# Down-projection in seven products of 256 columns in the second pass, with combinations made by GpSimd and SyncE in source order

## The chip, the cores and the metric

The kernel runs on one core of one Trainium2 chip. The core has TensorE (PE in the profile, its weight loads PEld), VectorE (DVE), ScalarE (ACT), GpSimd (POOL), SyncE (SP, which here issues the DMA transfers) and the DMA engines. Each engine works through its own instructions in order, and semaphores make one engine wait for another. The metric is the device time of one execution in microseconds; less is better.

## The reference

A transformer block on 2048 rows of 512: adaptive layer norm, attention of 32 query heads on 8 cached key/value heads over the last 512 cached positions, a gated residual, a second adaptive layer norm, and a gated feed-forward with F = 1792:

```python
def _B_ref(x, w_gate, w_up, w_down):
    return (_gelu(x @ w_gate) * (x @ w_up)) @ w_down
...
h = _layernorm(x, axis=-1) * (1 + ca) + sa
x = x + ga * _A_ref(h, A_k_cache, A_v_cache, A_wq, A_wo)
h = _layernorm(x, axis=-1) * (1 + cb) + sb
x = x + gb * _B_ref(h, B_w_gate, B_w_up, B_w_down)
```

Inputs and output are float32.

## The kernel before, in words

**Numbers.** Every matmul works on float16. A float32 operand is split in a high half (a ScalarE copy) and a low half (the difference, on VectorE or GpSimd), and a product is three matmuls: low by high, high by low, high by high (`mm3`, L85 to L88).

**Order.** Up to the first feed-forward sets, the program is a table of due positions: `at(position, function)` puts work there, and the block under `tc.manual_schedule()` (from L1383) runs the positions in turn; inside it every engine's instructions keep the order in which the source makes them. After it, the feed-forward loop (L1478 to L1494) makes its instructions in a similar order, but the framework's scheduler then orders each engine's queue, SyncE's included, by times of its own. `T` is the number of the attention's steps; positions T − 18 and so on are counted from its end.

**Feed-forward.** The hidden width is cut into blocks of 128, taken in pairs: NP = 7 pairs, two passes over them. The first pass (n = 0 to 6) does rows 0 to 1023, the second (n = 7 to 13) rows 1024 to 2047. Each n has two sets, q = 2n for the gate and q = 2n + 1 for the up projection. A set multiplies 1024 rows by 256 weight columns as a 2 × 2 block product in seven products (Winograd's form of Strassen), each of 6 matmuls of 512 columns: 42 matmuls. `ORDER` is the order of the seven. Three PSUM chains take them: `fa` (tag `s`, 2 buffers; `qa`, 1 buffer, for q = 0), `fb` and `fc` (tag `acc`, NACC = 5 buffers). The left combinations of the activations are tiles b11, b21, b22 and t1 to t4. Those of the second half of the rows are made in sets 7 to 10: SyncE loads four blocks (`combos`, L466), GpSimd makes differences (L478) and low halves (L343), ScalarE high halves (L339). The right combinations of the weights were made once, during the attention, and wait in DRAM (`store`, L310 to L312); `set_fetch` (L1094) and `fetch` (L314, L315) bring them back, four tiles a set, in buffers w0, w1, w2 and x3 of two each.

**After a product.** `keep` (L783 to L785) copies a chain from PSUM with ScalarE; VectorE adds two parts (L1161). For a gate set `gelu` runs on 128 × 512: square on ScalarE (L1168), VectorE (L1171), tanh on ScalarE (L1174), VectorE (L1178). For an up set VectorE multiplies by the gate (L1189), ScalarE takes the high half (L1191), VectorE the low (L1192): the tiles `at`, for keys 11, 21, 12 and 22 (two blocks of hidden columns by two quarters of the rows).

**Down-projection.** For each n `y_tasks` (L840 to L856) makes eight tasks, one for each row tile of 128: 2 × 3 matmuls of 512 columns in a bank `py`, with the scaled weight blocks `wo` (two a pair, fetched from what `prep_wd`, L1277, stored), and one VectorE addition onto `acc` (L852). They wait in `nexty`; `y_next` (L1444) takes one after products 1, 2, 5 and 6 of the next sets. The eight `acc` tiles are a half's rows. When the first pass is done with a row tile, `f_final` (L1473) stores it to the output and loads the second half's tile in its place.

**The seam with the attention.** `attn_final` (L858) stores each finished row tile `y` (L860) and loads the tile that is to come next in `acc` (L94). `ln_tile` (L420) loads a row tile `xs` from `y` (L427) for the second layer norm: statistics on VectorE (L352, L354, L356), the normalised rows (L434), transposes on TensorE (L439, `pln`), scaled copies (L447), stores of them (`hs`).

Of the kernel before, what the change touches and what calls it, by code (L numbers as in the profile page):

```python
# [63 lines left out]
def block_kernel(ctx: ExitStack, tc: tile.TileContext, x, kT, v, wq, wo, wg, wu, wd, cT, wc, wm, out):  # L64
# [709 lines left out]
    def banks(st, tags):  # L774
        def bk(k):
            def get():
                if k not in st:
                    st[k] = bank(*tags[k])
                return st[k]
            return get  # L780
        return bk
# [360 lines left out]

    NP = NF // 2
    NQ = 4 * NP
    B, A, G = {}, {}, {}

    def set_srcs(q):
        n, m = divmod(q, 2)
# [6 lines left out]
    def f_items(q, hold=None):  # L1155
        n, m = divmod(q, 2)
        st = {}
        done = set()

        def add(k, src):  # L1160
            nc.vector.tensor_tensor(st[k], st[k], st[src], op=ALU.add)  # L1161

        def gelu(key, src):
            b = {}

            def square():
                b["sq"] = pool.tile([P, QB], F32, tag="k", name="sq", bufs=2)
                nc.scalar.activation(b["sq"], src, AF.Square, scale=col("finv", f_scale(q)))  # L1168

            def inner():  # L1170
                nc.vector.scalar_tensor_tensor(b["sq"], b["sq"], 1.0 / GELU_A, src, op0=ALU.add, op1=ALU.mult)  # L1171

            def tanh():
                nc.scalar.activation(b["sq"], b["sq"], AF.Tanh, scale=col("tsc", f_scale(q)))  # L1174

            def outer():
                dst = tmp("fg") if key == "21" else src
                nc.vector.scalar_tensor_tensor(dst, b["sq"], 1.0, src, op0=ALU.add, op1=ALU.mult)  # L1178
                G[n, key] = dst

            return square, inner, tanh, outer

        def result(key, src):
            if m == 0:
                for step in gelu(key, src):
                    step()
            else:
                g = G.pop((n, key))
                nc.vector.scalar_tensor_tensor(g, g, 0.5 * GU, src, op0=ALU.mult, op1=ALU.mult)  # L1189
                t = pair("ot", "at", NOT)  # L1190
                nc.scalar.activation(t[:, 0, :], g, AF.Copy)  # L1191
                nc.vector.tensor_tensor(t[:, 1, :], g, t[:, 0, :], op=ALU.subtract)  # L1192
                A[n, key] = t
# [30 lines left out]
        return with_posts(("f", q), 2 + q // (2 * NP), banks(st, tags), after)  # L1224

    def f_spread_at(q):
        return (lambda m: f_spread(f_scale(q), m)) if q < 2 * NP else None
# [79 lines left out]
    for n in range(NP):  # L1307
# [1 line left out]
        prep_set(2 * n, b)  # L1309
        prep_set(2 * n + 1, b + 13)  # L1310
        prep_wd(n, b + 18)
    for q, ps_ in ((0, (T - 18, T - 17, T - 16, T - 15)), (1, (T - 8, T - 7, T - 3, T))):
        for k, pos in zip((0, 3, 2, 1), ps_):
            at(pos, lambda q=q, k=k: set_fetch(("f", q), ("f", q), k))

# [41 lines left out]
    def pushes(u, y):  # L1357
# [79 lines left out]
    def all_of(ts):  # L1437
        for g, post in ts:
            g()
            if post:  # L1440
                post()
                run(("d", now[0] + 1))

    def y_next():  # L1444
        if nexty:
            all_of(nexty.pop(0))

    ORDER = (1, 2, 6, 7, 5, 4, 3)

    def f_at(q, k, *fns):  # L1450
        at(("f", q, k), *fns)

    for n in range(2 * NP):
        for k in range(2):
            f_at(2 * n + 1, 2 * k, lambda n=n, k=k: WO.update({("f", n, k): fetch(("wd", n % NP, k), get_wo())}))
    for q in range(2, NQ):
# [16 lines left out]
    def f_final(ti):  # L1473
        nc.sync.dma_start(rows_of(out, ti), acc[ti])
        if ti < 2 * QT:
            load_acc(ti + 2 * QT, y1[ti + 2 * QT])

    f_done = {(0, k) for k in ORDER} | {(1, 1), (1, 2), (1, 6)}  # L1478
    for q in range(NQ):
        n, m = divmod(q, 2)  # L1480
        its = items(NG + q) if q < 2 else f_items(q)
        for k, pk in enumerate(ORDER):
            if (q, pk) not in f_done:
                all_of(its[pk])
            run(("f", q, k))
            if k in (1, 2, 5, 6):
                y_next()
        if m == 1:
            for qi, (a, b) in enumerate((("11", "21"), ("12", "22"))):
                for i in range(QT):  # L1490
                    nexty.append(y_tasks((2 * (n // NP) + qi) * QT + i, [lambda n=n, a=a: A[n, a], lambda n=n, b=b: A[n, b]],
                                         [("f", n, 0), ("f", n, 1)], col("dysc", n % NP), f_final if n % NP == NP - 1 else None))
    while nexty:
        y_next()  # L1494
    assert not later, list(later)


# [32 lines left out]
```

## Time and profile before

| | |
|---|---|
| runs | 1783.33, 1782.06, 1777.99 us |
| median | 1782.06 us |
| the profiled execution's own time | 1783.9 us |
| its span in the trace | 1782.1 us |
| its mean granted TensorE clock | 0.998 |
| HBM read, written | 133.83 MB, 59.90 MB |

A row of a group reads: line, engine, operation, output <- inputs, partitions × elements and types, count; after the bar the group's busy time in us and the mean duration of one in ns; after the second bar the engine's idle time just before these instructions, and what ended most of it. A row of a timeline has start and duration in us; a bracket at its end holds the idle time before and its releaser. A row of the chain of waits has start, duration and piece; "issue" is time in which the engine waited for nothing that the profile shows. Matmuls are pipelined, so their starts tell more than their durations. The attention ends, and the feed-forward takes the whole TensorE, at about 1346 us.

### The profile page before, as it was taken

To read this page: it belongs to the slowest core of one execution; us is meant where nothing else is said; L and a number is where in the kernel's file an instruction comes from. 1 tells how busy PE (TensorE), PEld (TensorE's weight loads), DVE (VectorE), ACT (ScalarE), POOL (GpSimd) and SP (SyncE) were. 2 spreads that over 40 slices of the span, in tenths; PEclk is the share of its full clock that TensorE was granted. 3 is DMA by queue.
4 is the path that set the end of the run, shared out by engine and by line. 5 is a ranking of instruction groups with operands and counts; after the bars stand their busy time and mean duration, and the time that the engine had idled before them with its cause. 6 is when DMAs were issued, how large, how long until landed. Compare 5 with 4: busy or idle time off the path is not lost.

```text
span 1782.1 us, 26030 instructions
## 1 busy us (share of the span) xinstructions
PE 1735.6 (97%) x8112; PEld 796.0 (45%) x8114; DVE 1442.5 (81%) x2517; ACT 1211.1 (68%) x2814; POOL 874.2 (49%) x1095
## 2 busy tenths in 40 slices
PE   7899999999999999999999999999999999999999
PEld 5444444444444444444444444444444444444444
DVE  7888888888888888888887888787885758676676
ACT  6877787878878777687877777777773455344342
POOL 4879878776788863236575375464420023000000
PEclk9999999999999999999999999999999999999999
DMA  7999999999999989999999999999985643252321
GB/s 232 197 189 236 204 224 207 222 214 206 218 211 210 211 175 182 228 223 212 217 208 211 237 203 212 212 196 203 187 184 141 215 126 99 73 177 84 86 69 56
DMA packets 663274, 329.71 MB, mean 185 GB/s; under 512 B 553184, under 2 KB 575968, under 8 KB 663136
## 3 DMA queue, kind: packets, MB, share of 16 engines
q1 hardware_dynamic: 662848, 327.53, 80.0%
q8 instruction: 64, 1.05, 0.3%
q14 instruction: 74, 0.61, 0.1%
q10 hardware_dynamic: 288, 0.52, 0.1%
HBM read 133.83 MB, written 59.90 MB: 109 GB/s over the span
## 4 chain that ended last, share of the span: by engine, by line
PE 67%; DVE 14%; ACT 7%; POOL 4%; DMA 4%; issue 4%; SPq 1%; POOLq 0%; ACTq 0%; DVEq 0%
PE py L86 7%; PE py L88 7%; PE py L87 7%; PE ps L86 4%; PE ps L88 4%; PE ps L87 4%; PE po L86 4%; PE po L88 4%; PE po L87 4%; DVE p L901 3%; DVE nm L875 3%; PE fa L86 2%; PE fa L88 2%; PE fa L87 2%; ACT ee L884 2%
## 5 line engine op out<-in xcount | busy, mean ns | idle before, releaser
L884 ACT ACTIVATE ee<-ps,nm 128x512 f32<-128x512 f32 x512 | 350.8, 685 | 244.6 <-DVE nm L875 234.6
L901 DVE SCALAR_TENSOR_TENSOR p<-ee,rr,p 128x512 f16<-128x512 f32 x512 | 464.8, 908 | 0.2
L875 DVE TENSOR_REDUCE nm<-ps 128x1 f32<-128x512 f32 x512 | 348.7, 681 | 67.2 <-PE ps L88 65.8
L896 ACT ACTIVATE p<-ee,rr 128x512 f16<-128x512 f32 x512 | 365.5, 714 | 12.8 <-DMA pt<-p 11.9
L86 PE MATMUL ps<-k,qt 128*128 128x512 f16 x512 | 194.3, 380 | 21.5 <-DVE qt L644 15.2
L86 PE MATMUL po<-pt,v 128*128 128x512 f16 x512 | 194.0, 379 | 2.8 <-DVE p L901 1.3
L86 PE MATMUL py<-wo,ot 128*128 128x512 f16 x512 | 194.1, 379 | 2.1 <-DVE ot L644 2.0
L88 PE MATMUL ps<-k,qt 128*128 128x512 f16 x512 | 194.2, 379 | 0.0
L87 PE MATMUL ps<-k,qt 128*128 128x512 f16 x512 | 194.2, 379 | 0.0
L88 PE MATMUL py<-wo,ot 128*128 128x512 f16 x512 | 194.0, 379 | 0.0
L87 PE MATMUL py<-wo,ot 128*128 128x512 f16 x512 | 194.0, 379 | 0.0
L88 PE MATMUL po<-pt,v 128*128 128x512 f16 x512 | 194.0, 379 | 0.0
L87 PE MATMUL po<-pt,v 128*128 128x512 f16 x512 | 194.0, 379 | 0.0
L892 DVE RECIPROCAL rr<-rr 128x2 f32<-128x2 f32 x256 | 41.5, 162 | 118.0 <-ACT rr L889 116.6
L87 PEld LDWEIGHTS <-w 128*128 128x128 f16 x728 | 71.4, 98 | 91.7 <-issue 7.6
L88 PEld LDWEIGHTS <-w 128*128 128x128 f16 x728 | 71.5, 98 | 86.8 <-issue 1.6
L86 PEld LDWEIGHTS <-w 128*128 128x128 f16 x728 | 71.4, 98 | 86.4 <-issue 1.3
L852 DVE SCALAR_TENSOR_TENSOR acc<-py,dysc,acc 128x512 f32<-128x512 f32 x112 | 81.7, 746 | 34.6 <-PE py L88 32.1
L362 POOL TENSOR_TENSOR rs<-rs,nhalf 128x1 f32<-128x1 f32 x32 | 19.2, 599 | 168.6 <-DVE rs L356 166.0
L884 ACT ACTIVATION_READ_ACCUMULATOR ee<-ps,nm 128x1 f32 x512 | 100.7, 197 | 0.0
L852 DVE SCALAR_TENSOR_TENSOR acc<-py,ysc,acc 128x512 f32<-128x512 f32 x128 | 94.6, 739 | 2.5 <-PE py L88 2.5
L86 PE MATMUL py<-wo,at 128*128 128x512 f16 x224 | 84.9, 379 | 3.0 <-DVE acc L852 1.9
(263 smaller groups left out, 3818.8 us busy)
## 6 DMA issues: line engine op xcount, KB each, us to landing
w<-kept SPq DMA_DIRECT2D x123, 256.0 KB, 3.1
wo<-kept SPq DMA_DIRECT2D x60, 256.0 KB, 3.2
raw<-in_wo SPq DMA_DIRECT2D x56, 256.0 KB, 3.5
kept<-stage SPq DMA_DIRECT2D x56, 256.0 KB, 3.5
kept<-w SPq DMA_DIRECT2D x39, 256.0 KB, 3.3
rw<-in_wq SPq DMA_DIRECT2D x38, 256.0 KB, 3.8
hs<-hf SPq DMA_DIRECT2D x32, 256.0 KB, 2.7
pt<-p SPq DMA_TRANSPOSE x512, 3.6
```

Of the source, the lines that this page charges most:

```text
L86: nc.tensor.matmul(ps, llo, rhi, start=first, stop=False, skip_group_check=chain)
L87: nc.tensor.matmul(ps, lhi, rlo, start=False, stop=False, skip_group_check=chain)
L88: nc.tensor.matmul(ps, lhi, rhi, start=False, stop=last, skip_group_check=chain)
L362: nc.gpsimd.tensor_tensor(st["rs"], st["rs"], nhalf, op=ALU.pow)
L852: nc.vector.scalar_tensor_tensor(acc[ti], st["p"], by, acc[ti], op0=ALU.mult, op1=ALU.add)
L875: nc.vector.tensor_reduce(nm, E[t]["ps"], axis=AX.X, op=ALU.max, negate=True)
L884: nc.scalar.activation(e, E[t]["ps"], AF.Exp, bias=E[t]["nm"], scale=1.0, accum_out=sm[:, t % 2:t % 2 + 1])
L892: return lambda: nc.vector.reciprocal(r, r)
L896: nc.scalar.activation(p16[:, 0, :], E[t]["e"], AF.Copy, scale=E[t]["r"])
L901: nc.vector.scalar_tensor_tensor(p16[:, 1, :], E[t]["e"], E[t]["r"], p16[:, 0, :], op0=ALU.mult, op1=ALU.subtract)
```

## The change

The down-projection of n = 7 to 12 (`seven(n)`) (two quarters of the rows by two hidden blocks, times two hidden blocks by two halves of 256 output columns) becomes a 2 × 2 block product in seven products too. Products are 128 × 256; each of the seven is 2 × 2 × 3 = 12 matmuls, 84 for an n where there were 48 of 512 columns. They run in two groups (x = 0, 1), each with two row tiles of either quarter of the rows: 6 matmuls a product and group.

- *Left combinations.* After the up set's product "12", `y_sums` makes four sums of 512 columns on GpSimd, then four splits (ScalarE copy, GpSimd difference), due after products of the next set: s1 to s4. The product with the gate goes into the up part's tile or a `qt` tile instead of the gelu's tile; "12" is not split on VectorE.
- *Right combinations.* `wd_combined(n)` for n = 0 to 5 in the first pass loads the two raw blocks again, scales them with GpSimd (a gate tile and two multiplications), makes four differences of 256 columns and two splits on it, and stores two tiles. In the second pass four `wo` tiles are fetched for such an n instead of two.
- *After the products.* Three of seven ("keep") are copied from PSUM by ScalarE with the scale into a tile `yk` and added to `acc` by GpSimd, two additions of 256 columns each; the other additions, of 256 columns too, stay on VectorE but are put off to behind the next task's matmuls (`defer`). For an n that is `seven` that makes 6 ScalarE copies, 12 GpSimd additions and 16 VectorE additions.
- *Banks.* Chain `fa` takes its bank in turn from `qa`, `s`, `s` (`chain_tag`), and chain a of the down-projection shares that turn.
- *Order.* SyncE's whole program is put in source order (the line `manual_schedule(engines={... SP})`); the other engines are ordered as before. Set 2 and the first `wo` tiles are fetched near the attention's end, the loads of `acc` for the second half are put off (`load_later`), and `y_next` runs after every product once n > 7 or while such loads wait.

The last pair (n = 13) and the whole first pass keep the plain down-projection. TensorE's instructions in all: 216 matmuls more.

```diff
+    def seven(n):
+
+        return NP <= n < 2 * NP - 1
...
+    def y_sums(n):
+        g11, g21, g12, g22 = (R.pop((n, k)) for k in ("11", "21", "12", "22"))
+        nc.gpsimd.tensor_tensor(g22, g12, g22, op=ALU.add)
+        nc.gpsimd.tensor_tensor(g12, g11, g12, op=ALU.subtract)
+        nc.gpsimd.tensor_tensor(g11, g22, g11, op=ALU.subtract)
+        nc.gpsimd.tensor_tensor(g21, g21, g11, op=ALU.subtract)
...
+            nc.scalar.activation(t[:, 0, :], src, AF.Copy)
+            nc.gpsimd.tensor_tensor(t[:, 1, :], src, t[:, 0, :], op=ALU.subtract)
...
+        for i, (k, src) in enumerate(((0, g22), (1, g11), (3, g21), (2, g12))):
+            at(("f", 2 * n + 2, 1 + i), lambda k=k, src=src: split(k, src))
...
-        tags = {"a": ("s", "fa", 2) if q else ("qa", "fa", 1), "b": ("acc", "fb", NACC), "c": ("acc", "fc", NACC)}
+        tags = {"a": chain_tag, "b": ("acc", "fb", NACC), "c": ("acc", "fc", NACC)}
...
+        return (("qa", "fa", 1), ("s", "fa", 2), ("s", "fa", 2))[(chains[0] - 1) % 3]
...
+    for k in range(2):
+        at(T - 1 + 2 * k, lambda k=k: WO.update({("f", 0, k): fetch(("wd", 0, k), get_wo())}))
+    for q, ps_ in ((0, (T - 18, T - 17, T - 16, T - 15)), (1, (T - 8, T - 7, T - 3, T)), (2, (T + 2, T + 3, T + 4, T + 5))):
...
+    ctx.enter_context(tc.manual_schedule(engines={mybir.EngineType.SP}))
...
     def y_next():
         if nexty:
+            fns = defer[:]
+            defer.clear()
             all_of(nexty.pop(0))
+            for fn in fns:
+                fn()
+        if len(load_later) > 2 or load_later and not nexty:
+            t = load_later.pop(0)
+            load_acc(t, y1[t])
...
+    YPROD = {1: ("a", "11", 0, 0, "keep", 0, 0), 2: ("b", "21", 1, 0, "add", 0, 0), 5: ("c", "s1", 2, 0, "add", 1, 1),
+             6: ("a", "s2", 3, 1, "keep", 0, 1), 3: ("c", "s4", 1, 1, "add", 0, 1), 7: ("a", "s3", 2, 1, "keep", 1, 1),
+             4: ("a", "22", 3, 0, "add", 1, 0)}
+
+    def y_seven(n, x):
...
+            for ii in range(2):
+                sl = slice((2 * x + ii) * P, (2 * x + ii + 1) * P)
+                mm3(st[ch][:, 256 * ii:256 * ii + 256], A[n, a][:, 0, sl], A[n, a][:, 1, sl], w[:, 0, rs], w[:, 1, rs],
+                    k in (1, 2, 5) and ii == 0, k in (2, 3, 4) and ii == 1, True)
...
+            if what == "keep":
+                src = pool.tile([P, 512], F32, tag="rw", name="yk", bufs=NRW)
+                nc.scalar.activation(src, st[ch], AF.Copy, scale=by)
+            for ii in range(2):
...
+                if what == "keep":
+                    nc.gpsimd.tensor_tensor(t, t, s_, op=ALU.add)
+                else:
+                    defer.append(lambda t=t, s_=s_: nc.vector.scalar_tensor_tensor(t, s_, by, t, op0=ALU.mult, op1=ALU.add))
...
+    def wd_combined(n, q):
...
+        def combine():
+            tt(st[0][:, l], st[0][:, r], st[0][:, l])
+            tt(st[0][:, r], st[1][:, r], st[0][:, r])
+            tt(st[1][:, r], st[1][:, r], st[0][:, l])
+            tt(st[1][:, l], st[1][:, l], st[1][:, r])
...
+        def keep_it(k):
+            store(("wd", n, 2 + k), st["o", k])
+
+        for d, fn in enumerate((lambda: (load(0), load(1)), nop, gate, lambda: scaled(0), lambda: scaled(1), combine,
+                                lambda: parts(0), lambda: parts(1), nop, lambda: keep_it(0), lambda: keep_it(1))):
+            f_at(q + d // 7, d % 7, fn)
...
+    for n in range(1, 2 * NP):
+        for k in range(4 if seven(n) else 2):
+            f_at(2 * n + 1, 1 + k if seven(n) else 2 * k, lambda n=n, k=k: WO.update({("f", n, k): fetch(("wd", n % NP, k), get_wo())}))
+    for n in range(NP - 1):
+        wd_combined(n, 2 * n + 3)
+    for q in range(3, NQ):
...
-            load_acc(ti + 2 * QT, y1[ti + 2 * QT])
+            load_later.append(ti + 2 * QT)
...
-            if k in (1, 2, 5, 6):
+            if n > NP or k in (1, 2, 5, 6) or load_later:
                 y_next()
-        if m == 1:
+        if m == 1 and seven(n):
+            f_at(q + 1, 2, lambda n=n: nexty.extend(y_seven(n, 0) + y_seven(n, 1)))
+        elif m == 1:
```

More of the change, by code (lines that the diff above doesn't have):

```diff
@@ L1188, in result @@
                 g = G.pop((n, key))
[L1189 to L1193, printed above, removed]
+                dst = src if seven(n) and key != "21" else get_qt32() if seven(n) else g
+                nc.vector.scalar_tensor_tensor(dst, g, 0.5 * GU, src, op0=ALU.mult, op1=ALU.mult)
+                R[n, key] = dst
+                if not seven(n) or key != "12":
+                    t = pair("ot", "at", NOT)
+                    nc.scalar.activation(t[:, 0, :], dst, AF.Copy)
+                    nc.vector.tensor_tensor(t[:, 1, :], dst, t[:, 0, :], op=ALU.subtract)
+                    A[n, key] = t
+                if seven(n) and key == "12":
+                    y_sums(n)
         def out_(key, src):
@@ L1451, in f_at, with load, gate, scaled @@
         at(("f", q, k), *fns)
[L1453 to L1456, printed above, removed]
+    def wd_combined(n, q):
+        st = {}
+        l, r = slice(0, 256), slice(256, 512)
+        def load(k):
+            st[k] = raw("raw")
+            nc.sync.dma_start(st[k], wd[(2 * n + k) * P:(2 * n + k + 1) * P, :])
+        def gate():
+            st["g"] = pool.tile([P, D], F32, tag="gs", name="gs", bufs=1)
+            pool_ts(st["g"], rows[5], col("dsc", n))
+        def scaled(k):
+            nc.gpsimd.tensor_tensor(st[k], st[k], st["g"], op=ALU.mult)
+        def tt(o, a, c):
+            nc.gpsimd.tensor_tensor(o, a, c, op=ALU.subtract)
+        def combine():
[3 more added lines that the diff above has]
+            tt(st[1][:, l], st[1][:, l], st[1][:, r])
+        def parts(k):
+            st["o", k] = pair("p16", "wdc", NP16)
+            halves(st["o", k], st[k])
+        def keep_it(k):
[9 more added lines that the diff above has]
+    for q in range(3, NQ):
         for k, at_ in ((0, 2), (3, 2), (1, 3), (2, 4)):
@@ L1494, in block_kernel @@
         y_next()
+    for fn in defer:
+        fn()
     assert not later, list(later)
```

30 lines of the change are left out of this document (27 added, 3 removed).

## The prediction

> **What bounds the kernel now.** I read the page's totals first, then the engines by stretch from the last attention step on, then single waits.
>
> ```profile
> span 1782.1 us, 26030 instructions
> PE 1735.6 (97%) x8112; PEld 796.0 (45%) x8114; DVE 1442.5 (81%) x2517; ACT 1211.1 (68%) x2814; POOL 874.2 (49%) x1095
> ```
>
> TensorE (PE) bounds the whole, so every term below is either TensorE work or TensorE waiting. By stretch (start to end, length; then busy time and count of PE, PEld, DVE, ACT and POOL; then clock and DMA):
>
> ```profile
> 1345.00:1375.00 30.00, 27.13 (x118) 11.90 (x119) 15.16 (x25) 9.83 (x16) 0.95 (x1) 0.94 0.43 116
> 1375.00:1410.00 35.00, 32.80 (x154) 15.02 (x153) 25.11 (x48) 11.24 (x22) 2.74 (x5) 1.00 0.66 212
> 1410.00:1455.00 45.00, 45.00 (x222) 22.06 (x221) 32.92 (x55) 26.01 (x54) 2.25 (x3) 1.00 0.47 139
> 1455.00:1490.00 35.00, 32.03 (x146) 13.90 (x145) 23.12 (x31) 17.08 (x31) 28.46 (x21) 1.00 0.43 132
> 1490.00:1757.00 267.00, 267.00 (x1239) 121.06 (x1238) 186.34 (x284) 108.20 (x171) 0.00 (x0) 1.00 0.31 91
> 1757.00:1782.10 25.10, 20.82 (x96) 8.98 (x94) 16.65 (x25) 5.75 (x10) 0.00 (x0) 1.00 0.23 84
> ```
>
> From 1490 to 1757 TensorE never waits: 267.00/1239 = 0.2155 us for a 512-column matmul. Fewer columns there shorten the run one for one. GpSimd (POOL) does nothing there; VectorE is busy 70%, ScalarE 41%. A pair of feed-forward sets with a down-projection is 84 + 48 = 132 matmuls, 28.4 us. Ahead of 1490 TensorE idles 2.87 + 2.20 + 0 + 2.97 = 8.0 us: the only other time to be won.
>
> **The matmuls.** In six of seven pairs of the second pass 84 matmuls of 256 columns replace 48 of 512. Neither pass has a 256-column product with this shape, so its price is bounded: half of 0.2155 is 0.108; if the weight load cannot hide, 0.108 + 0.098 = 0.206.
>
> ```profile
> 1447.83 0.38 PE L88 MATMUL py<-wo,at 128*128 128x512 f16 x1
> 1448.04 0.60 PE L439 MATMUL pln<-ident,xs 128*128 128x128 f32 x4
> 1448.48 0.38 PE L86 MATMUL fb<-b,w 128*128 128x512 f16 x1
> L88 PEld LDWEIGHTS <-at 128*128 128x128 f16 x153 | 15.0, 98 | 18.0
> ...
> ```
>
> (0.38 is pipelined duration; starts count.) The nearest row is the four transposes, each with weights of its own: 1448.48 − 1448.04 = 0.44, or 0.11 each, so weights do change every 0.11 us. I take 0.109, just over half. Each n: 48 × 0.2155 − 84 × 0.109 = 1.19; six make **−7.1** (−7.7 at half). Break-even is 10.34/84 = 0.123.
>
> The Trainium skill, "TensorE: Matmul & The Clock Gate", under "The mechanism", says that a weight load overlaps running matmuls only when it goes to another row group, and these loads fill all rows. Here the 98 ns loads stand between 512-column matmuls at 0.2155, so they are hidden; the trace disagrees, and no run here shows 256 columns. By the rule each of them would take 0.206, the last rival's case.
>
> **SyncE in source order, and the waits early in the first pass.** Before, VectorE held normalisations whose rows had not arrived:
>
> ```profile
> 1346.40 0.76 DVE acc L852
> ...
> 1348.22 2.75 DMA y<-acc
> ...
> 1351.04 3.02 DMA xs<-y
> ...
> 1354.08 0.70 DVE bn L352
> ```
>
> ```profile
> 1360.22 0.38 PE L88 MATMUL fa<-b,w 128*128 128x512 f16 x1
> 1362.94 0.58 PE L86 MATMUL fa<-t,w 128*128 128x512 f16 x1 [2.33 <-ACT fg L785]
> 1363.32 0.63 PE L87 MATMUL fa<-t,w 128*128 128x512 f16 x1
> ```
>
> ```profile
> 1397.09 5.27 DMA xs<-y
> ...
> 1405.64 0.67 DVE acc L852
> ...
> 1406.36 0.66 PE pln L439 x4
> ```
>
> While bn waited for xs, the gelu steps queued behind it on VectorE, ScalarE's copies behind those, and TensorE stood 2.33 us; the matmuls after that start 0.43 apart instead of 0.2155, and seven of them lose 1.5. At 1402 the same wait costs the 2.20 idle of 1375 to 1410. In the changed program's order the first bn stands behind attention's last adds, and y8 to y15 stores and all eight acc loads stand ahead of the xs loads on SyncE. So gelu no longer queues behind a bn that waits; I leave 0.7 for copies late by themselves: 2.33 + 1.5 + 2.2 − 0.7 = **−5.3**. Bounds: −6.5, if all of the idle goes, to 0, if the later xs loads (sixteen transfers further back) give it back.
>
> At the turn of the passes, the acc loads and output stores precede set fetches in SyncE's order: TensorE waits there for nothing now; sixteen issues of 0.42 us are spread over pairs; I take **+0.7** (0 to 2).
>
> ```profile
> 1385.08 0.42 SPq L94 DMA_DIRECT2D acc<-y  x1
> ```
>
> **GpSimd in the first pass.** For six pairs it scales and combines two wd blocks. By the rows of such forms:
>
> ```profile
> L1245 POOL TENSOR_TENSOR rw<-rw 128x256 f32<-128x256 f32 x56 | 48.5, 866 | 4.1
> L1298 POOL TENSOR_TENSOR raw<-raw,gs 128x512 f32<-128x512 f32 x14 | 18.8, 1344 | 0.6
> L153 POOL TENSOR_TENSOR stage<-rw,stage 128x512 f16<-128x512 f32 x42 | 55.0, 1310 | 3.5
> L152 POOL TENSOR_SCALAR stage<-rw 128x512 f16<-128x512 f32 x42 | 30.5, 725 | 2.5 <-DMA kept<-stage 0.2
> ...
> L478 POOL TENSOR_TENSOR cb<-cb 128x512 f32<-128x512 f32 x8 | 11.5, 1437 | 27.7 <-DMA cb<-hs 27.7
> L343 POOL TENSOR_TENSOR t<-cb,t 128x512 f16<-128x512 f32 x8 | 11.0, 1379 | 0.0
> ```
>
> 0.73 (gate) + 2 × 1.344 + 4 × 0.866 + 2 × (0.725 + 1.310) = 11.0 us a pair. Elsewhere GpSimd is near idle, but in sets 7 to 10 it also makes the second half's combinations: a pair's four L478 and seven L343, 15.4, so 26.4 of 28.4. SyncE meanwhile waits in its queue for the combined pieces' halves before it may issue the next set's w0, then the following cb loads; ScalarE waits for t1 to t4. A fetch needs 3.1 us. Laying the rows end to end, set 7's fetch is in time, set 8's 0.5 late, set 9's 2 to 4, while the 2.97 idle of today partly falls in the same places. I take **+2** (0 to +9, if set 9's lateness is paid, GpSimd overruns, and the clock halves once).
>
> ```profile
> w<-kept SPq DMA_DIRECT2D x123, 256.0 KB, 3.1
> ```
>
> **The second pass's helpers.** Each n now gives GpSimd four sums (1.344), four splits (1.310) and twelve 256-column adds (0.866): 21.0 of the new 27.2 us; ScalarE ten copies more, less one split.
>
> ```profile
> L852 DVE SCALAR_TENSOR_TENSOR acc<-py,dysc,acc 128x512 f32<-128x512 f32 x78 | 56.9, 747 | 26.9 <-PE py L88 24.5 <-DMA x<-kept 1.6
> L1192 DVE TENSOR_TENSOR at<-fg,at 128x512 f16<-128x512 f32 x38 | 26.2, 689 | 9.6 <-ACT at L1191 8.3
> L1171 DVE SCALAR_TENSOR_TENSOR sq<-sq,fg 128x512 f32<-128x512 f32 x29 | 20.0, 688 | 3.6 <-ACT sq L1168 3.6
> ...
> L785 ACT ACTIVATE fg<-fa 128x512 f32<-128x512 f32 x29 | 17.2, 594 | 46.4 <-PE fa L88 46.4
> ```
>
> Ten copies add some 5.9 us to ScalarE's 11.5 (108.20/267 of 28.4): hidden. VectorE changes eight adds of 0.747 for sixteen of 256 columns, between 0.37 and 0.75; in the ratio of GpSimd's two sizes (0.866/1.344) 0.48. 7.7 − 6.0 − 0.69 = +1.0 on 19.9: hidden.
>
> Not hidden by totals alone is the handover. After a pair's last product VectorE needs three steps (3 × 0.69 = 2.1), then GpSimd two sums, the keep adds that stand between in its order, and the split of s1. In the changed program's order the pairs have 0, 2, 2, 0, 4 and 4 adds there, the last also a third sum. With two: 2.1 + 2 × 1.344 + 2 × 0.866 + 1.310 = 7.8; over the pairs 6.1, 7.8, 7.8, 6.1, 9.6, 10.9. Up to its first matmul on s1 TensorE's order holds, for the third pair, 36 matmuls of 512 columns and 24 of 256, 36 × 0.2155 + 24 × 0.109 = 10.4; counted so, 7.3, 8.2, 10.4, 7.8, 11.0, 11.7. The margins are 0.4 to 2.6, the later operands' wider, ScalarE's copies of s not in them: I take 0.4 a pair, **+2.4** (0 to +12, if each is 2 late).
>
> **Tail.** Now one 0.75 add follows the last matmul. The plain last pair remains, but with deferred adds of the pair before it ahead on VectorE and two more y tasks drawn earlier or later:
>
> ```profile
> 1778.08 0.23 PE py L88
> ...
> 1778.34 0.75 DVE acc L852
> ```
>
> Two 256 and two 512 adds may stand there, 2 × 0.48 + 2 × 0.75 − 0.75 = 1.7: **+1.5** (0 to 2).
>
> **Sum.** −7.1 − 5.3 + 0.7 + 2 + 2.4 + 1.5 = −5.8 on the profiled execution. Its span of 1782.1 and 1.8 us around it make 1783.9, 1.84 over the median 1782.06; so 1782.06 − 5.8 = **1776.3 us**.
>
> **Rivals.** *SyncE's order gives nothing.* The attention's stores and acc loads delay xs by as much as bn was moved. For: at 1397 the xs transfer itself took 5.27 us, and more transfers now share that time. Against: the bn that waits no longer stands ahead of the gelu steps at all. The −5.3 vanishes: 1781.6.
>
> *GpSimd and VectorE slow each other, and what GpSimd makes comes late* (the slower case). Where both work, VectorE's step L1171 takes longer, and GpSimd's difference has a long end (min/median/max):
>
> ```profile
> L1171 DVE SCALAR_TENSOR_TENSOR sq<-sq,fg 128x512 f32<-128x512 f32 x12 | 9.9, 821 | 1.9 <-ACT sq L1168 1.7
> L478 POOL TENSOR_TENSOR cb<-cb x27: 1262/1271/1781, 103.6 to 1482.6; 128x512 f32<-128x512 f32 x27
> ```
>
> 821/688 = 1.19 and 1781/1271 = 1.40. With these on VectorE's and GpSimd's parts the six handovers become 8.1, 10.5, 10.5, 8.1, 13.0 and 14.8, late by 0.8, 2.3, 0.1, 0.3, 2.0 and 3.1: 8.6 instead of 2.4. The three of 2 us and more are as long as the stall that lost the clock at 1362: 3 × 1.5 = 4.5. In sets 7 to 10 GpSimd's 11.0 becomes 15.4, 2.4 over the 28.4 in two pairs: 4.8. Together 15.5: 1792. It decides from where GpSimd is slowed by about 1.1. Against: in the busy stretch L478 has a mean of 1.437, only 1.13 of 1.271, and my prices are means that hold some of it.
>
> The Trainium skill, "SBUF — State Buffer", under "Who interferes with whom", has a VectorE instruction with two SBUF inputs and a GpSimd instruction that reads SBUF exclude each other for their whole length. The two rows above agree in kind. By it the splits and products of VectorE, twelve of 0.69, add 8.2 to GpSimd's 21.0 of 27.2, which no longer fits: the rival's time or more.
>
> *Weight loads stand between 256-column matmuls*: 504 × (0.206 − 0.109) = +49, 1825.
>
> **How the numbers follow.** The forecast has 0.50, by itself 1770 to 1781 (the first pass's and the handover's terms at nothing and the matmuls at half, or one of the two up by 4); SyncE's order idle 0.15; the mutual slowing 0.27; weight loads 0.04; 0.04 for a gain above all bounds. Some 0.3% (5.35 us) is what a measurement can tell here: faster is below 1776.7, slower above 1787.4. Of the forecast's 0.50, 0.32 lies below; with the 0.04 and 0.02 of the idle order, faster 0.38. Same: 0.18 of the forecast, 0.13 of the idle order, 0.02 of the slowing: 0.33. Slower: 0.29. The range, 1766 to 1793, leaves out the weight loads and the upper part of the slowing.
>
> **What would show it.** Right: 256-column matmuls start 0.108 to 0.110 apart; no 2 us stall near 1360 and 1402 and a full clock; GpSimd at 70 to 80% in the second pass with its 512 sums near 1.34; TensorE idle under 4 us there, ahead of as operands. Wrong: waits of TensorE on w fetches or on ScalarE t around sets 8 to 10 beyond 4 us, GpSimd's sums above 1.5, VectorE's 0.69 steps above 0.8, starts above 0.123 apart, or a clock under 1.00 after 1490.

## The result, and the profile after

The changed kernel takes 1793.08 us (median of 6 runs, 1789.39 to 1795.03) against 1781.97: a ratio of 1.0065 (95% interval 1.005 to 1.008), 0.65% slower where 0.3% faster was forecast, and just past the far end of the range (1766 to 1793). The profiled execution has a span of 1791.8 us. Its page, totals:

```profile
span 1791.8 us, 26801 instructions
...
PE 1736.0 (97%) x8330; PEld 817.1 (46%) x8330; DVE 1473.9 (82%) x2559; ACT 1241.7 (69%) x2868; POOL 1068.2 (60%) x1281
```

The same view by stretch as before the change; the first pass now ends near 1600:

```profile
1345.00:1375.00 30.00, 29.04 (x134) 13.10 (x135) 15.02 (x23) 9.52 (x16) 0.00 (x0) 1.00 0.47 132
1375.00:1410.00 35.00, 35.00 (x169) 16.65 (x168) 26.26 (x47) 15.21 (x29) 6.65 (x8) 1.00 0.64 212
1410.00:1455.00 45.00, 40.54 (x195) 19.10 (x194) 35.12 (x58) 21.43 (x43) 19.36 (x22) 1.00 0.38 123
1455.00:1520.00 65.00, 57.02 (x241) 24.14 (x239) 45.47 (x56) 27.78 (x46) 49.84 (x41) 0.92 0.43 142
...
1600.00:1660.00 60.00, 57.01 (x333) 32.09 (x331) 43.16 (x69) 32.95 (x54) 35.28 (x35) 1.00 0.45 149
1660.00:1765.00 105.00, 102.68 (x621) 60.32 (x619) 85.18 (x138) 60.73 (x100) 78.64 (x76) 1.00 0.29 95
```

The first two rows are won: 0.96 us of idle where there were 2.87 + 2.20, and the full clock. The next two lose 4.46 + 7.98, the second of them with a clock of 0.92. The second pass, which never waited, now idles 2.99 + 2.32. TensorE's waits in the first pass, from its timeline:

```profile
1361.03 0.38 PE L86 MATMUL fa<-t,w 128*128 128x512 f16 x1 [0.69 <-ACT fg L785]
...
1418.82 0.39 PE L86 MATMUL fa<-b,w 128*128 128x512 f16 x1 [1.50 <-DMA w<-kept]
...
1446.74 0.39 PE L86 MATMUL fa<-b,w 128*128 128x512 f16 x1 [1.34 <-DMA w<-kept]
...
1478.39 0.58 PE L86 MATMUL fa<-t,w 128*128 128x512 f16 x1 [3.38 <-ACT u L785]
...
1514.90 0.61 PE L86 MATMUL fa<-b,w 128*128 128x512 f16 x1 [2.54 <-DMA w<-kept]
```

The wait of 2.33 us before the gelu result near 1360 is down to 0.69. New are waits for weights (`w<-kept`) that the kernel before does not have; from 1345 to 1600 they make 5.8 of the 14 us that TensorE waits, and waits for ScalarE's copies (L785) make 6.4. SyncE's timeline shows why the weights come late:

```profile
1410.06 0.57 SPq L427 DMA_DIRECT2D xs<-y  x1
1415.62 0.32 SPq L312 DMA_DIRECT2D kept<-wdc  x1
1415.99 0.42 SPq L315 DMA_DIRECT2D w<-kept  x1
...
1457.22 0.33 SPq L312 DMA_DIRECT2D kept<-wdc  x1
1457.64 1.05 SPq L315 DMA_DIRECT2D w<-kept  x2
1458.78 1.89 SPq L475 DMA_DIRECT2D cb<-hs  x4
...
1461.19 15.63 SPq L1544 DMA_DIRECT2D raw<-in_wd  x2
...
1495.61 14.44 SPq L1544 DMA_DIRECT2D raw<-in_wd  x2
1510.09 0.43 SPq L315 DMA_DIRECT2D wo<-kept  x1
1510.57 0.43 SPq L315 DMA_DIRECT2D w<-kept  x1
```

From 1410.6 to 1415.6 SyncE issues nothing: the store of a combined block waits for GpSimd, and the fetch that TensorE waits for at 1418 stands right behind it. At 1457 the same kind of store stands ahead of the loads for the second half's combinations. At 1461 and 1495 two loads of raw blocks take 15.63 and 14.44 us to issue: the ring of five raw buffers holds four blocks of those combinations, so the second load waits until ScalarE and GpSimd let one go, and the fetch at 1510.57 is the one that TensorE waits for until 1514.90.

The longest wait, 3.38 us until 1478.39, is for a ScalarE copy, and two things stand ahead of that copy. ScalarE waits 7.0 us for the late `cb` loads, until 1464.41 (4.5 us, until 1459.67, before). Then VectorE's gelu steps, which ScalarE's copies follow, are slow while GpSimd makes the combinations:

```profile
1468.98 1.43 DVE L1197 SCALAR_TENSOR_TENSOR sq<-sq,fg 128x512 f32<-128x512 f32 x1 [0.44 <-ACT sq L1194]
1470.34 1.75 DVE L1216 SCALAR_TENSOR_TENSOR fg<-fg,fu 128x512 f32<-128x512 f32 x1
```

With GpSimd idle, in the second pass of the kernel before, such steps take 0.69 us. After the waits at 1478 and 1515 the matmuls start 0.43 us apart for a while instead of 0.2155: half clock.

The second pass by groups, 1600 to 1765 (mean ns behind the busy time):

```profile
L1527 POOL TENSOR_TENSOR acc<-acc,yk 128x256 f32<-128x256 f32 x62 | 51.3, 852 | 79.9 <-ACT yk L1522 79.9
L1529 DVE SCALAR_TENSOR_TENSOR acc<-py,dysc,acc 128x256 f32<-128x256 f32 x64 | 29.0, 476 | 9.0 <-POOL acc L1527 8.3 <-PE py L88 0.4
L1197 DVE SCALAR_TENSOR_TENSOR sq<-sq,fg 128x512 f32<-128x512 f32 x17 | 18.3, 1076 | 8.2 <-ACT sq L1194 8.2
...
L1167 POOL TENSOR_TENSOR as<-u,as 128x512 f16<-128x512 f32 x12 | 15.6, 1307 | 0.0
...
L1187 DVE TENSOR_TENSOR fg<-fg,fc 128x512 f32<-128x512 f32 x11 | 7.5, 677 | 3.1 <-ACT fg L785 3.1
...
L1156 POOL TENSOR_TENSOR u<-u,u 128x512 f32<-128x512 f32 x6 | 8.1, 1344 | 2.5 <-DVE u L1216 2.5
...
L1197 DVE SCALAR_TENSOR_TENSOR sq<-sq,fa 128x512 f32<-128x512 f32 x5 | 3.4, 677 | 0.0
```

GpSimd's sums, splits and additions have on the mean about the durations that the forecast gave them (1.35, 1.34 and 0.85 us). VectorE's first gelu step on two SBUF tiles (`sq<-sq,fg`, 688 ns before) takes 1076; the same step with its second input in PSUM (`sq<-sq,fa`) takes 677, and so does the addition with one input in PSUM (L1187). The first gelu step is the worst case: over all VectorE's steps of 128 × 512 with both inputs in SBUF the mean is 924 ns in this stretch, for 687 before.

### The profile page after: what moved, and what is told of

Read it like the earlier page. It is cut to its first block, busy times and chain, and to the rows that moved or that the text cites. A ratio compares the mean times of both kernels' runs of the same rounds, so it can differ in the third digit from the quotient of the medians.

```text
span 1791.8 us, 26801 instructions
## 1 busy us (share of the span) xinstructions
PE 1736.0 (97%) x8330; PEld 817.1 (46%) x8330; DVE 1473.9 (82%) x2559; ACT 1241.7 (69%) x2868; POOL 1068.2 (60%) x1281
## 4 chain that ended last, share of the span: by engine, by line
PE 50%; DVE 19%; ACT 10%; POOL 10%; issue 6%; DMA 4%; SPq 1%; DVEq 0%; POOLq 0%; ACTq 0%
DVE p L901 5%; PE py L86 5%; PE py L87 5%; PE py L88 5%; DVE nm L875 4%; PE ps L86 4%; PE ps L88 3%; PE ps L87 3%; PE po L86 3%; PE po L88 3%; PE po L87 3%; ACT ee L884 3%; ACT p L896 2%; DVE qt L644 2%; DVE acc L852 2%
## 5 line engine op out<-in xcount | busy, mean ns | idle before, releaser
L1527 POOL TENSOR_TENSOR acc<-acc,yk 128x256 f32<-128x256 f32 x72 | 59.7, 854 | 90.2 <-ACT yk L1522 90.2
L362 POOL TENSOR_TENSOR rs<-rs,nhalf 128x1 f32<-128x1 f32 x32 | 19.6, 612 | 156.4 <-DVE mv L354 85.2
L229 POOL TENSOR_TENSOR lw<-lw,half__86 128x1 f32<-128x1 f32 x37 | 21.9, 593 | 112.1 <-DVE lw L179 112.0
```

What stands on the lines that cost most here:

```text
L229: nc.gpsimd.tensor_tensor(out, out, half_, op=ALU.pow)
L1527: nc.gpsimd.tensor_tensor(t, t, s_, op=ALU.add)
```

## The experiments

Each ran beside the kernel before on its chip; a ratio is to that one, with its 95% interval, and differences between kernels are taken from ratios, times 1780 us.

### The first pass

**Without the combined blocks.**

```diff
-    for n in range(NP - 1):
-        wd_combined(n, 2 * n + 3)
...
-        ... fetch(("wd", n % NP, k), get_wo())
+        ... fetch(("wd", n % NP, k % 2), get_wo())
```

> The changed kernel without the combined weight blocks: their loads, GpSimd work and stores in the first pass are left out, and the second pass fetches the two plain blocks in their place (four fetches a pair, as before; that part of the output is not the reference's). Theory 1 (in the first pass SyncE, in source order, stands behind loads and stores that belong to GpSimd's combined blocks, and set fetches and the combinations of the second half come late): TensorE's losses between 1345 and 1600 us fall from about 20 us, slow clock included, to 5 or less, and the time to 1778 to 1781. Theory 2 (SyncE's source order alone does it, by stores that wait for ScalarE): the waits for w near 1417 and 1445 stay, and the time is above 1787. Theory 3 (the second pass loses nearly all): above 1788.

1776.52 us, 0.9977 (0.9963 to 0.9992): 15.7 us less than the changed kernel, a little more than theory 1 asked. Theories 2 and 3 fall by the time. One wait for w is left, 2.28 us near 1440; the plain kernel in the same order has it too, with 1.42. What remains, by stretch:

```profile
1345.00:1582.00 237.00, 234.03 (x1100) 108.04 (x1099) 167.08 (x265) 105.94 (x184) 34.42 (x30) 1.00 0.42 131
1582.00:1747.00 165.00, 158.44 (x945) 91.75 (x943) 127.44 (x205) 93.07 (x153) 112.88 (x110) 1.00 0.34 115
```

3.0 us of idle in the first pass, at full clock, but 6.6 in the second: that loss is one of its own.

**Without SyncE's order.**

```diff
-    ctx.enter_context(tc.manual_schedule(engines={mybir.EngineType.SP}))
```

> The changed kernel without that one line: SyncE's queue of the feed-forward is ordered by the framework's scheduler again. Theory 1 (the queue is what makes fetches late; GpSimd has the time): waits for w in sets 3 to 11 go and the time falls by 6 to 10 us, to 1783 to 1787. Theory 2 (GpSimd's own backlog makes the combinations late whatever SyncE does): ScalarE's waits for t1 to t4 stay, and the time is within 3 us of the changed kernel, 1790 to 1796.

1781.56 us, 1.0005 (0.9995 to 1.0016): 10.7 us less, more than theory 1 asked. GpSimd has the same work in both, so most of what that work costs comes only when a queue in source order stands behind it. Against the plain kernel without the order (0.9999, below) and with 7.3 us for the cheaper matmuls (below), blocks and sums together cost some 8 us here, for 22.5 with the order.

**Stores later.**

```diff
-    lambda: parts(0), lambda: parts(1), nop, lambda: keep_it(0), lambda: keep_it(1))):
+    lambda: parts(0), lambda: parts(1), nop, nop, nop, nop, lambda: keep_it(0), lambda: keep_it(1))):
```

> The changed kernel with the two stores of each combined block pair four products later, behind the next set's fetches in SyncE's order. If the stores that wait for GpSimd are what holds the fetches: the waits for w near 1417, 1445 and 1492 go, the loads for the second half's combinations start 3 to 5 us earlier, and the time falls by 5 to 8 us to 1785 to 1788. If the loads of the raw blocks hold SyncE (they wait for one of five buffers of the ring that the combinations' loads share): the 14 us stands at 1461 and 1495 and the wait for w near 1512 stay, and the time falls by less than 3 us.

1787.84 us, 1.0042 (1.0028 to 1.0056): 4.1 us less by the ratios, just clear of the noise. The wait for w near 1417 goes, but a wait of 2.1 us, put down to a layer norm step, comes in its place, and the wait for the fetch behind the raw loads (the two take 14.9 us to issue, until 1504.2) grows to 4.5. Both readings have a part.

**Another ring for the raw blocks.**

```diff
-            st[k] = raw("raw")
+            st[k] = pool.tile([P, 512], F32, tag="rw", name="rawd", bufs=NRW)
```

> The changed kernel with the raw blocks of the combined weights in the ring of two buffers that is free in the first pass, not in the ring of five that the combinations' loads use; the stores stay where they are. If the ring holds SyncE: its stands of 14 us at 1461 and 1495 go, the wait for w near 1512 goes with 2.7 us and its slow clock, and the time falls by 3 to 6 us to 1787 to 1790. If the stores do: less than 2 us.

1790.39 us, 1.0054 (1.0034 to 1.0073): 2.0 us less, which the intervals do not tell from nothing. The wait near 1512 is gone, but one of 4.2 us for w stands at 1488, and SyncE issues that fetch at 1489.7, right behind a store of a combined block that waits for GpSimd: with the ring mended the store decides there.

**Both, and other sets.**

```diff
-    for n in range(NP - 1):
-        wd_combined(n, 2 * n + 3)
+    for n, q in zip(range(NP - 1), (3, 4, 5, 11, 12, 13)):
+        wd_combined(n, q)
```

with the two edits above.

> The changed kernel with all three mended: later stores, the other ring, and the combined blocks made in sets 3, 4, 5, 11, 12 and 13 instead of 3, 5, 7, 9, 11 and 13, so not while GpSimd makes the second half's combinations. If the first pass loses only by these: its losses come down to what is left without the combined blocks at all (about 5 us) and the time to 1776 to 1779. If GpSimd's work itself costs by slowing VectorE: 1780 to 1785.

1784.28 us, 1.0026 (1.0013 to 1.0040): 6.9 us less, but 8.7 us above the run without the blocks. The timelines around 1415 show what is left:

```profile
1411.96 1.61 POOL L153 TENSOR_TENSOR wdc<-rawd,wdc 128x512 f16<-128x512 f32 x1
1413.53 0.99 POOL L362 TENSOR_TENSOR rs<-rs,nhalf 128x1 f32<-128x1 f32 x1
...
1418.24 0.39 PE L86 MATMUL py<-wo,at 128*128 128x512 f16 x1 [1.74 <-DVE rs L356]
```

L362 is the layer norm's power on a 128 × 1 column. It stands among GpSimd's long operations, and VectorE needs it to normalise `xs`. But ahead of the wait shown VectorE does not stand for it: it works from 1401.5 to 1428.1 without a gap of more than 0.15 us, and all its waits for L362 between 1345 and 1590 are two, 3.2 us together (one of 0.7 without the blocks). What fills VectorE is slow steps:

```profile
1403.51 1.75 DVE L1216 SCALAR_TENSOR_TENSOR fg<-fg,fu 128x512 f32<-128x512 f32 x1
1405.19 1.76 DVE L1204 SCALAR_TENSOR_TENSOR fg<-sq,fg 128x512 f32<-128x512 f32 x1
```

In the run without the blocks the same two steps, at 1403.76 and 1404.36, take 0.69 and 0.68. Over 1400 to 1600 VectorE's steps of 128 × 512 on two SBUF tiles have a mean of 963 ns here and 759 there.

**The small step left out.**

```diff
-            ln_power(st)
+            if gen < 3:
+                ln_power(st)
```

on the kernel just told.

> The kernel with later stores, the other ring and moved blocks (sets 3, 4, 5, 11, 12, 13), without GpSimd's power of the second layer norm's row tiles in the first pass, a step of 128 x 1 (so these rows are not normalised as in the reference). If what that kernel still loses near 1416, 1423 and 1429 is this small step queued between GpSimd's long ones: these three waits (1.9, 1.3 and 1.2 us) go, and the time falls by 4 to 6 us, to about 1779. If it is VectorE, slowed while GpSimd works, or SyncE's stores of normalised rows: less than 2 us.

1778.97 us, 0.9986 (0.9973 to 0.9999): 7.1 us less. The three waits named are gone; one of 2.96 us for w at 1420 and small ones are left. So leaving the step out wins most of what remained, but the run does not show how. Its 7.1 us have an interval of 3.3 either way (the trace is of its slowest execution, 1781.86). The chain of a row tile is shorter by the step's own 0.55 to 0.99 us. And VectorE's order changes with it: near 1408 one step stands between the statistics and the `xs` step, instead of five. VectorE's slow steps are fewer but still there (a mean of 851 ns). How much belongs to the step's place in GpSimd's queue, and how much to VectorE, stays open; in the run without the blocks the step can cost no more than the 3.0 us of idle that are left there.

**All blocks in sets 11 to 16.**

```diff
-    for n, q in zip(range(NP - 1), (3, 4, 5, 11, 12, 13)):
+    for n, q in zip(range(NP - 1), (11, 12, 13, 14, 15, 16)):
```

on the kernel with the three edits above, and with the small step.

> The same kernel with the combined blocks in sets 11 to 16: behind all layer norm steps and all combinations of the first pass, and each still ahead of its fetch. If the first pass's loss is a matter of what GpSimd's work stands ahead of, not of its amount: 1776 to 1778, as without the combined blocks. If the amount counts: 1781 or more.

1789.25 us, 1.0048 (1.0028 to 1.0069): the second reading came, and the time is no better than with sets 3, 4, 5, 11, 12 and 13 (3.9 us more, 4.4 either way). The first pass waits little up to 1580, but the last blocks now run in the second pass, where GpSimd has its sums: waits of 3.3 us for w at 1589 and of some 2.5 us for ScalarE at 1614, 1662 and 1692. The amount counts as soon as it meets other work.

### SyncE's order and what comes with it

**The order alone, on the kernel before.**

```diff
+    ctx.enter_context(tc.manual_schedule(engines={mybir.EngineType.SP}))
     with tc.manual_schedule():
```

> The kernel before with one line more: SyncE's whole program in source order. Theory 1 (the order by itself is harmless or helps): 1776 to 1780, without the 2.3 us wait at 1360 and the 2 us wait at 1402. Theory 2 (the order by itself makes set fetches wait behind stores of normalised rows): 1783 to 1790, with waits of TensorE for w that the kernel before does not have.

1792.13 us, 1.0061 (1.0041 to 1.0080): the order by itself loses 11 us, a little more than theory 2 asked. The wait at 1402 goes, but the one near 1360 stays (2.67 us, until 1358.3). It is theory 2's mechanism with other stores than it named: TensorE waits 3.8 us for w near 1382, a fetch that stands behind stores of finished row tiles (L860) and loads of `acc` (L94), and longer near 1593, where SyncE's queue is:

```profile
1590.39 0.38 SPq L1475 DMA_DIRECT2D out_y<-acc  x1
1593.77 0.32 SPq L94 DMA_DIRECT2D acc<-y  x1
...
1594.62 0.42 SPq L315 DMA_DIRECT2D w<-kept  x1
```

```profile
1598.99 0.61 PE L86 MATMUL fa<-b,w 128*128 128x512 f16 x1 [5.62 <-DMA w<-kept]
```

The acc load must wait for the store of the tile that it replaces (3 us here), and the set fetch waits in the queue behind both. The changed kernel's `load_later` and earlier fetches are made for this.

**The rest of the change without the seven products.**

```diff
     def seven(n):
 
-        return NP <= n < 2 * NP - 1
+        return False
...
-    for n in range(NP - 1):
-        wd_combined(n, 2 * n + 3)
```

> The changed kernel with the plain down-projection in all pairs and without the combined blocks: SyncE in source order, the early fetches of set 2, the later acc loads, the bank rotation and the more frequent y tasks are left. If the order with these helpers is a gain by itself (the forecast's 5.3 us): 1775 to 1778. If the order is a loss of 11 us as in the kernel before with the order alone and the helpers don't mend it: above 1785. In between, 1779 to 1782: the helpers just pay for the order.

1775.84 us, 0.9980 (0.9971 to 0.9989): a gain of 3.6 us.

**The same without the order** (the line of SyncE's order taken out too).

> The same without SyncE's source order: the helpers alone. If the helpers, not the order, make the gain: 1775 to 1778. If they only mend what the order costs: 1779 to 1783, as the kernel before.

1780.32 us, 0.9999 (0.9989 to 1.0009). So the helpers alone are worth nothing, the order alone minus 11 us, both together 3.6. With the helpers alone the wait near 1360 is down to 1.24 us, with both to 0.68.

### The second pass

**Without sums and splits.**

```diff
 def y_sums(n):
...
-        nc.gpsimd.tensor_tensor(g22, g12, g22, op=ALU.add)
...
+        for k, key in (("s1", "11"), ("s2", "21"), ("s3", "22"), ("s4", "11")):
+            A[n, k] = A[n, key]
```

> The changed kernel without the four sums and four splits of each pair in the second pass; the products read the plain tiles in place of s1 to s4 (that part of the output is not the reference's). GpSimd keeps its twelve additions. Theory 1 (GpSimd's long operations slow VectorE's gelu steps and hold up the s operands): VectorE's step that takes 1.08 us between 1600 and 1765 falls to below 0.85, TensorE's losses there from 8.7 to about 3, and the time by 5 to 6 us to 1787 to 1788. Theory 2 (the GpSimd additions to acc, on which VectorE's additions to the same tiles wait, are what is lost): VectorE's 8 us of waits for them stay, and the time falls by 2 us at most, to 1791 or more.

1785.01 us, 1.0020 (1.0010 to 1.0029): 8.0 us less. TensorE's only wait of note from 1602 on is one of 1.0 us for w at the turn of the passes. By groups:

```profile
L1515 DVE SCALAR_TENSOR_TENSOR acc<-py,dysc,acc 128x256 f32<-128x256 f32 x70 | 31.4, 479 | 19.2 <-POOL acc L1513 16.0 <-PE py L88 3.3
L1183 DVE SCALAR_TENSOR_TENSOR sq<-sq,fg 128x512 f32<-128x512 f32 x18 | 13.9, 774 | 4.3 <-ACT sq L1180 4.1
```

The first gelu step falls to 774 ns, and the mean of VectorE's steps on two SBUF tiles from 924 to 724. VectorE waits twice as long for GpSimd's additions as before (16.0 us), and that costs nothing: theory 2 falls. The end of the program is shorter too: 1.2 us from the start of the last matmul to the end of the last addition, for 2.5 in the changed kernel.

**The sums alone left out** (the four sum lines taken out, the splits kept).

> The changed kernel without the four sums of each pair on GpSimd; the four splits stay and take the unsummed tiles (that part of the output is not the reference's). If the second pass loses by GpSimd's long operations as such, slowing VectorE and being late: half of the 8 us that the run without both won, so 3 to 5 us, 1787 to 1790, and VectorE's first gelu step between 774 and 1076 ns. If it loses by the chain of sums ahead of the splits: 6 to 8 us.

1788.25 us, 1.0045 (1.0028 to 1.0062): 3.6 us less, about half, but with an interval of 4.0 either way, which does not shut out the other reading. The first gelu step is at 763, below the range named; other steps stay slow, and the mean of all on two SBUF tiles is 843 ns, about half way from 724 (neither sums nor splits) to 924 (both). That speaks for GpSimd's long operations as such.

**GpSimd's additions given to VectorE.**

```diff
-                    nc.gpsimd.tensor_tensor(t, t, s_, op=ALU.add)
+                    defer.append(lambda t=t, s_=s_: nc.vector.tensor_tensor(t, t, s_, op=ALU.add))
```

> The changed kernel with the twelve additions of 256 columns per pair that GpSimd makes given to VectorE, put off like its own. It takes 10 us a pair from GpSimd and gives VectorE some 5.7. If VectorE's waits for GpSimd's additions to the same acc tiles and the slowed VectorE steps are what the second pass loses: its losses of 8.7 us fall to 4 and the time to 1788. If VectorE has no room (22 us and more of 27.2 a pair): losses grow, 1795 to 1805.

1804.52 us, 1.0130 (1.0108 to 1.0152): VectorE has no room. TensorE idles 13.3 us between 1600 and 1765, with waits of 2 to 4 us for VectorE's additions to free a bank.

**Neither the blocks' work nor sums and splits** (the edits of the first run of either pass together).

> The changed kernel without the combined blocks' work in the first pass and without the sums and splits of the second (its output is not the reference's in what these feed): the cheaper matmuls with nothing paid for them but the additions. If the matmul term is right (7.1 us) and these two are all that is lost beside it: 1768 to 1771. If the GpSimd additions and seam waits cost too: 1772 to 1776.

1767.72 us, 0.9939 (0.9927 to 0.9952), 7.3 us below the plain kernel in the same order (2.7 either way). In the second pass it idles as little as that one; here the row of the plain kernel and then of this one:

```profile
1582.00:1747.00 165.00, 164.32 (x762) 74.28 (x761) 113.89 (x172) 67.22 (x105) 0.00 (x0) 1.00 0.27 90
```

```profile
1582.00:1747.00 165.00, 164.25 (x1001) 97.93 (x1001) 121.69 (x218) 86.28 (x138) 55.53 (x70) 1.00 0.34 112
```

**Seven products for three pairs**, their blocks in sets 11 to 13.

```diff
-        return NP <= n < 2 * NP - 1
+        return NP + 3 <= n < 2 * NP - 1
...
-    for n, q in zip(range(NP - 1), (3, 4, 5, 11, 12, 13)):
+    for n, q in zip(range(3, NP - 1), (11, 12, 13)):
```

on the kernel with later stores, the other ring and moved blocks.

> The seven products for three pairs only (n = 10 to 12), their weight blocks combined in sets 11 to 13, where GpSimd has neither the layer norms' small steps nor the second half's combinations, with the later stores and the other ring. If what is lost grows with each pair's GpSimd work in the second pass (about 1 us a pair) and the first pass then loses nothing: 1775 to 1778, near the plain kernel in the same order. If GpSimd's work in sets 11 to 13 still delays something: above 1780.

1774.99 us, 0.9973 (0.9964 to 0.9982), the fastest version that leaves nothing out: 4.8 us below the kernel before. From the plain kernel in the same order (0.9980) it can't be told apart: for three pairs, too, the seven products bring no more than what goes with them takes.

## Why the prediction was wrong

Four of the runs part the change by ratios: order and helpers −3.6 us (0.9980); the cheaper matmuls, with their additions, −7.3 (0.9939); sums and splits +6.8 (0.9977); combined blocks +15.7 (1.0065). Each is the step from one run to the next, so they add up to the measured +11.6 (0.65%) in any case; each is uncertain by some 3 us.

**The matmuls, −7.1: right.** They start 0.11 us apart, 0.109 on the mean in the run with neither blocks nor sums:

```profile
1626.53 0.27 PE L86 MATMUL fa<-wo,at 128*128 128x256 f16 x1
1626.64 0.27 PE L87 MATMUL fa<-wo,at 128*128 128x256 f16 x1
1626.74 0.27 PE L88 MATMUL fa<-wo,at 128*128 128x256 f16 x1
```

The rival of weight loads in the open (0.206) is out. With it goes the rule of the Trainium skill ("TensorE: Matmul & The Clock Gate", "The mechanism") that weight loads overlap running matmuls only across row groups: the measurement decides against it. The same section of the Trainium skill also lets a load into the background weight buffer go ahead of running matmuls, which would fit.

**SyncE's order, −5.3 and +0.7: the size nearly, the reason in part.** Both early waits went, 2.33 us at 1360 to 0.69 and that at 1402 altogether, with the clock. But the prediction gave the gain to the order; the order alone leaves 2.67 us near 1360 and loses 11 us, above all behind stores of row tiles and acc loads, and only the put-off loads and early fetches make it a gain. Together −3.6 against −4.6. The seam's "+0.7 (0 to 2)" holds only with them: two waits of 0.69 us in the changed kernel, 6.3 us with the order alone.

**GpSimd in the first pass, +2 (0 to 9): this step failed.** It measured 15.7. The prediction added GpSimd's rows, found 26.4 of 28.4 us in sets 7 to 10 and "elsewhere GpSimd is near idle", and priced one late fetch. Its durations came nearly so (by the rows between 1400 and 1600, 11.6 us a pair for 11.0). What it had wrong is what GpSimd's work does to the other queues:

- *SyncE.* Near 1410, with GpSimd idle for 7 us shortly before, SyncE already stood 5 us at the first store. The second raw load stood 14 to 15 us, twice, on a ring that I had not counted (4 + 2 blocks on 5 buffers). By the run without the order and its plain partner, most of the loss needs SyncE's order.
- *VectorE.* Its steps on two SBUF tiles slow down here as in the second pass: a mean of 926 ns between 1400 and 1600, for 759 without the blocks. The prediction gave that only to its slower rival, and there by GpSimd's time.
- *The layer norm's small step* queued among the new operations, which I did not look for: VectorE waits 4.0 us for it in the changed kernel.

Mending the stores, the ring and the sets together gave back 6.9, leaving out the small step 7.1 more (with the reservations told there); 1.6 is left, within the noise. Without SyncE's order VectorE's steps are slow too (a mean of 865 ns), and little is lost; no run keeps SyncE's order and the blocks and takes VectorE's slowing away, so the share of each stays open. After the waits at 1478 and 1515 the clock was at half, 0.92 over 1455 to 1520; the prediction let it halve once, at the end of its range.

**The second pass, +2.4 (0 to 12): mis-sized, 6.8 to 8.0 (0.9977 − 0.9939, and 1.0065 − 1.0020).** Of that some 1.3 us is the longer tail, so 5.5 to 6.7 stand against +2.4. "+1.0 on 19.9: hidden" was wrong about VectorE: its count was right, not its durations. For the handover the prediction took 0.4 us a pair. In the changed kernel's trace TensorE waits for an `as` operand once, 0.43 us, and its other waits are for VectorE and ScalarE; but in four other runs with these sums (no order, later stores, no small step, three pairs) it waits 1.7 to 2.6 us for `as`. So the margins are as thin as the prediction said, and which step is late differs from kernel to kernel.

**The tail, +1.5: right.** From the start of the last matmul to the end of the last addition there are 2.47 us, against 1.17 before (1777.92 to 1779.09). The rows before and after the change:

```profile
1777.92 0.38 PE L88 MATMUL py<-wo,at 128*128 128x512 f16 x1
```

```profile
1786.27 0.38 PE L88 MATMUL py<-wo,at 128*128 128x512 f16 x1
```

```profile
1786.54 0.88 DVE L1529 SCALAR_TENSOR_TENSOR acc<-fa,dysc,acc 128x256 f32<-128x256 f32 x2 [2.20 <-PE fa L88]
1787.34 1.40 DVE L852 SCALAR_TENSOR_TENSOR acc<-py,dysc,acc 128x512 f32<-128x512 f32 x2
```

In the runs without the sums and splits it is 1.2 us, so it goes with them and not with the 256-column matmuls.

**The slower rival** gave 1792, near the time, but in good part by luck. It was right that VectorE slows beside GpSimd, with 1.19 for a measured 1.56 (first gelu step; 1.34 over all steps on two SBUF tiles). But it slowed GpSimd by 1.40, where the means stayed near the forecast's prices, and took most of its time from late handovers; two thirds of the measured loss lie in the first pass, most of it behind SyncE's order, which the rival did not have.

## What to carry to other kernels

Before an engine that is idle gets new work, list what stands behind each of its results in the queues of the others: in a DMA queue kept in source order, a store that waits for 10 us of work on an engine that was idle before (1405.31 to 1415.60 here) holds every fetch behind it. Count the buffers of every ring that a moved load shares, look for small steps of other work on that engine, and give VectorE's steps on two SBUF tiles their price beside a busy GpSimd (0.92 us here), not beside an idle one (0.69). An order written out by hand is worth nothing or worse without the moves that suit it, so the two are measured together and apart.

## What the runs showed of the hardware

Beside GpSimd's operations, VectorE's steps of 128 × 512 on two SBUF inputs took 924 ns on the mean for 687 (the first gelu step 1076), those with one input in PSUM stayed at 678 (683 before). One by one (min/median/max, changed kernel, 1600 to 1765):

```profile
L1197 DVE SCALAR_TENSOR_TENSOR sq<-sq,fg x17: 677/992/1730, 1609.7 to 1761.8; 128x512 f32<-128x512 f32 x17
L1156 POOL TENSOR_TENSOR u<-u,u x6: 1261/1272/1716, 1612.4 to 1750.8; 128x512 f32<-128x512 f32 x6
```

Some of GpSimd's operations are longer too, by about 0.45 us, and they were in the kernel before (1.262 to 1.781 us for L478), so the forecast's prices held that already. That agrees with the Trainium skill ("SBUF — State Buffer", "Who interferes with whom"), in which VectorE instructions with two SBUF inputs meet GpSimd's and either side can block. The size of it is the case's own.
